# Another sequence and other rooms for the second part of an attention, dense and soft-MoE kernel

## The chip, the cores and the metric

The kernel runs on one core of one Trainium2 chip. The metric is the device time of one execution in microseconds (us).

## The reference

Three layers stand one behind the other.

- Attention in which a query sees only the keys of its own cluster. The shapes are 2 batches, 8 heads, 768 tokens, 64 columns, with 16 centroids per head. Query and key are each assigned to the centroid with the largest cosine.
- A dense layer on 1536 tokens x 512 columns: `h = x @ w_in` (512 x 2048), `g = h * clip(h + 3, 0, 6) / 6`, `x = g @ w_out` (2048 x 512).
- A soft mixture of 8 experts with 4 slots each: logits by `phi` (512 x 32), a softmax over the tokens for the input of the slots, two matrices per expert (512 x 1024 and 1024 x 512, relu between), and a softmax over the slots for the output.

```python
logits = x @ phi
d = np.exp(logits - logits.max(0, keepdims=True)); d /= d.sum(0, keepdims=True) + 1e-09
slot_input = d.T @ x                                  # 32 slots x 512
slot_out[e] = np.maximum(slot_input[e] @ w1[e], 0.0) @ w2[e]
c = np.exp(logits - logits.max(1, keepdims=True)); c /= c.sum(1, keepdims=True) + 1e-09
return (c @ slot_out).astype(np.float32)              # 1536 x 512
```

## The kernel before

Batch and head make 16 heads in all (head 8 to 15 belong to batch 1), and the tokens make 12 tiles of 128 (tile 6 to 11 belong to batch 1). The heads run one after the other; the dense layer of a tile can only start when all heads of its batch are done. So the dense layer of batch 0 runs beside the heads of batch 1, and the dense layer of batch 1 behind the heads.

Every piece of the work is a Python generator that issues instructions up to its next `yield`; such a stretch is a step. `ev` (L270) numbers the generators, and `flush` (L273) issues all steps in the sequence of `ORDER`, a list of 2706 numbers of generators written out as text: the n-th time that a number stands there, the n-th step of that generator is issued. Each engine executes its own instructions in the order in which they were issued, and the DMA queues of SP and ScalarE take their transfers in that order too. The text `ORDER` is thus the order of work on every engine. `Rooms` (L206) gives a tile a fixed buffer among those of its kind by its name: `ROOMS` lists `name:number`; a new tile in a room waits until the readers of the former one are done. A tile whose name has no number, or another text than the others, gets a buffer of its own kind.

The generators of which this document speaks are these; `name(arguments)` with a number behind it (`.4`) is the step, counted from 0.

- `keep(n, m)` (L374) issues m filler matmuls of 256 columns (L377) into a tile kw that nobody reads.
- `cast_lo` (L427, transfer at L443) turns the low part of query and key of a head with a DMA on SP's queue; `as_mm` (L461, L467) multiplies the turned tile by the centroids. `maxr`, `scores`, `maxq` and `as_put` are other steps of a head.
- `hid(t, fb, part, parts)` (L745) multiplies tile t by a fourth of `w_in`; `act(t, f0, f1)` (L748) computes the dense layer's function on ScalarE, VectorE and GpSimd (L762, L764, L358, L368), and its step `.4` turns the result with a DMA on SP's queue (L773), or for tiles 6, 10 and 11 with TensorE (L782). `logits(t)` (L790, matmuls at L796 and L797) reads the turned tile; it is called the classifier of tile t here.
- `colmax`, `dweights`, `dispatch` (L814 to L862) keep a running softmax over the tokens and the input of the slots; `zsum` (L1246), `slot_in` (L1281) and `slot_t` (L1290) finish that input.
- `fetch` (L1048) issues the transfers of the experts' weights on SP's queue, two halves of 512 KB per number (`fetch4.1` is the second half of number 4; L1099), each into a room of memory that earlier tiles leave. The second matrices of the last four experts come in two parts of 352 and 160 columns (`PARTS`, L1057), of which the output's first and second part are made. The first fetches read `wos`, the converted `w_out`, which is stored to memory from ScalarE's queue before.
- `combine_weights` (L1304) computes the softmax over the slots on VectorE, ScalarE and GpSimd, and turns it in its step `.11` with twelve transposes of TensorE (L1340).
- `layer1` (L1408), `relu`, `turn` (L1432), `layer2` (L1447) and `layer2_part(p, i)` (L1462) are the experts' layers; `layer2_part` also scales its result (ScalarE L1474, VectorE L1476).
- `combine(p, b)` (L1368) makes the output of part p and batch b: matmuls (L1387), an eviction per piece by ScalarE (L1395) or VectorE (L1393), and the output transfers (L1398, L1401), of batch 0 on ScalarE's queue and of batch 1 on SP's.

Of the kernel before, what the change touches and what calls it, by code (L numbers as in the profile page):

```python
# [71 lines left out]
    "753 598 989 661 633 634 595 599 629 602 661 722 976 599 603 988 989 712 976 723 714 630 634 603 977 994 718 "  # L72
    "989 630 662 715 635 989 637 638 977 719 996 716 717 720 631 755 755 756 977 933 997 667 978 978 638 668 995 "
    "978 979 604 998 639 1002 632 632 636 636 640 1002 605 649 756 721 605 1002 1002 650 641 640 1000 724 642 642 "
    "999 645 643 725 650 726 979 726 1001 756 646 713 651 727 646 1003 644 644 647 728 713 671 1003 672 728 729 648 "
    "648 731 665 652 652 713 757 732 732 1008 1003 666 735 1022 669 653 757 733 989 976 663 654 736 654 1010 757 "
    "757 739 1009 758 736 737 758 670 673 759 740 730 730 740 1003 674 734 741 734 743 759 675 676 744 744 745 1011 "
    "677 677 738 1016 1016 1023 1024 1025 747 760 738 742 990 1026 1027 748 748 678 761 1028 771 742 990 765 746 "
    "990 749 679 991 682 679 746 750 750 683 772 683 991 826 680 763 684 767 766 751 821 686 768 681 991 752 664 "
    "764 769 664 752 681 685 690 687 687 664 770 992 1022 691 773 685 694 774 992 992 691 698 688 692 762 695 695 "  # L80
    "775 696 689 1119 762 689 699 693 775 762 776 693 699 777 777 697 1037 780 1037 697 993 1012 700 781 784 788 "
    "993 781 1002 1003 701 701 778 1029 779 782 785 785 779 783 783 789 792 796 990 786 789 793 793 790 787 787 797 "
    "797 794 702 798 1014 791 1013 791 795 795 799 1016 1016 703 1004 1004 1004 1004 1025 703 1027 1026 1015 1017 "
    "799 800 1029 801 1049 1044 801 1037 1017 1030 1005 1016 1017 1046 1031 1005 1005 1006 1006 1017 1037 1045 1038 "
    "1047 1048 1006 1007 1051 1058 1017 1048 1018 1048 1041 1048 1039 1052 1050 1018 1032 1018 1019 1053 1019 1019 "
    "1053 1028 1033 1059 1048 1053 1048 1048 1020 1018 1040 1020 1031 1024 1020 1053 1060 1061 1060 1053 1042 1053 "
    "1021 1060 1062 1034 1007 1053 1060 1054 1054 1063 1035 1054 1068 1063 1035 1063 1063 1055 1055 1069 1060 1055 "
    "1056 1063 1070 1056 1071 1056 1021 1057 1072 1043 1070 1023 1070 1036 1054 1070 1064 1064 1064 1073 1078 1109 "
    "1064 1033 1065 1073 1073 1073 1079 1065 1065 1109 1070 1066 1066 1066 1081 1073 1067 1032 1080 1080 1080 1057 "
    "1082 1074 1074 1074 1088 1080 1083 1083 1074 1034 1075 1083 1075 1089 1083 1075 1076 1076 1076 1067 1091 1110 "  # L90
    "1090 1090 1077 1080 1083 1092 1090 1084 1084 1090 1077 1084 1090 1090 1085 1093 1085 1085 1093 1093 1098 1111 "
    "1036 1093 1086 1086 1086 1099 1100 1090 1101 1101 1099 1087 1102 1101 1101 1093 1084 1093 1093 1099 1099 1104 "
    "1087 1101 1103 1105 1103 1103 1105 1103 1094 1099 1110 1094 1105 1094 1094 1099 1101 1099 1103 1095 1103 1105 "
    "1101 1095 1103 1105 1095 1105 1105 1106 1106 1106 1096 805 1127 1096 1096 1107 1107 1097 1097 1107 1108 1108 "
    "1133 1133 1106 1108 1133 1134 1143 1143 1133 1126 1143 1143 1143 1132 1135 1112 1112 1137 1139 1143 1140 1143 "
    "1143 1143 1143 1143 1143 1141 1113 1113 1141 1114 1114 1130 1141 1115 1115 1116 1144 1145 1111 1150 1155 1156 "
    "1117 1116 1117 1118 1118 1136 1151 1159 1159 1138 1136 1138 1146 1147 1147 1146 1148 1149 1157 1158 1165 1165 "
    "1152 1153 1154 1154 1154 1154 1154 1149 1148 1153 1142 1152 1154 1154 1154 1154 1142 1160 1143 1160 1154 1154 "
    "1154 1154 1154 1154 1154 1154 1154 1154 1154 1161 1142 1166 1166 1161 1142 1142 1167 1162 1163 1168 1167 1168 "
    "1169 1169 1169 1173 1169 1171 1171 1171 1171 1172 1174 1171 1171 1171 1171 1172 1172 1172 1172 1174 1171 1172 "  # L100
    "1172 1172 1172 1174 1174 1177 1177 1177 1177 1177 1176 1120 1176 1125 1128 1123 1176 1176 1176 1121 1122 824 0 "
# [31 lines left out]
)  # L133

ROOMS = (
    "acc_0:1 acc_1:1 acc_10:1 acc_11:0 acc_12:0 acc_13:0 acc_14:0 acc_15:1 acc_2:0 acc_3:1 acc_4:0 acc_5:1 acc_6:1 "
    "acc_7:0 acc_8:0 acc_9:0 al_1:0 al_10:0 al_11:1 al_2:1 al_3:2 al_4:0 al_5:1 al_6:2 al_7:0 al_8:1 al_9:2 as_0:0 "
    "as_1:1 as_10:0 as_11:1 as_12:1 as_13:0 as_14:1 as_15:1 as_2:0 as_3:0 as_4:0 as_5:1 as_6:0 as_7:1 as_8:0 as_9:1 "
    "cTp:2 cm_0:0 cm_1:1 cm_10:0 cm_11:0 cm_12:0 cm_13:1 cm_14:1 cm_15:1 cm_2:0 cm_3:1 cm_4:1 cm_5:0 cm_6:0 cm_7:1 "
# [1404 lines left out]
```

## Time and profile before

| what | value |
| --- | --- |
| median of 3 runs | 443.02 us (442.69 to 443.47) |
| profiled execution | 442.37 us |
| span of its instructions | 440.5 us, so 1.87 us lie around it |
| granted TensorE clock over the span | 0.997 |

One execution was taken by the profiler; the median belongs to three other ones. A time in a row is counted from the start of the span. PE is TensorE, PEld its weight loads, DVE VectorE, ACT ScalarE, POOL GpSimd, SP the engine that only issues transfers; ACTq and SPq are the queues on which transfers are issued. The duration of a matmul in a row contains its way through the array, so successive matmuls overlap, and what one takes of the engine is the distance from its start to the next one's. `Lnnn` is a line of the kernel, `a<-b` says that tile a is written from tile b, `xN` is a number of instructions, and what stands in square brackets at the end of a row of a timeline is the idle time of the engine before it and what ended it. The DMA share of a stretch is the mean busy share of the core's 16 DMA engines; it can come out a little over 1.

### The profile page before, as it was taken

To read this page: it belongs to the slowest core of one execution; us is meant where nothing else is said; L and a number is where in the kernel's file an instruction comes from. 1 tells how busy PE (TensorE), PEld (TensorE's weight loads), DVE (VectorE), ACT (ScalarE), POOL (GpSimd) and SP (SyncE) were. 2 spreads that over 40 slices of the span, in tenths; PEclk is the share of its full clock that TensorE was granted. 3 is DMA by queue.
4 is the path that set the end of the run, shared out by engine and by line. 5 is a ranking of instruction groups with operands and counts; after the bars stand their busy time and mean duration, and the time that the engine had idled before them with its cause. 6 is when DMAs were issued, how large, how long until landed. Compare 5 with 4: busy or idle time off the path is not lost.

```text
span 440.5 us, 11801 instructions
## 1 busy us (share of the span) xinstructions
PE 423.7 (96%) x4906; PEld 276.4 (63%) x4906; DVE 271.4 (62%) x479; ACT 310.5 (70%) x508; POOL 248.9 (57%) x213
## 2 busy tenths in 40 slices
PE   7899999999999999999999999999999999989993
PEld 5577778776887556565656566765454445652652
DVE  5999999999867678465577476713343344650322
ACT  7799999997999887888878788885344454510112
POOL 6557588966566586568776779887133323310000
PEclk9999999999999999999999999999999999999998
DMA  7998958996795999425884607975998997999998
GB/s 258 294 199 215 259 91 223 224 237 233 244 214 99 246 256 220 130 53 107 136 208 92 172 9 214 239 257 106 207 343 181 271 220 252 329 350 400 373 306 274
DMA packets 129909, 96.28 MB, mean 219 GB/s; under 512 B 99648, under 2 KB 115008, under 8 KB 129856
## 3 DMA queue, kind: packets, MB, share of 16 engines
q1 hardware_dynamic: 125936, 89.74, 79.6%
q10 hardware_dynamic: 3920, 5.80, 3.7%
q8 instruction: 38, 0.62, 0.6%
q14 instruction: 15, 0.12, 0.1%
HBM read 64.06 MB, written 7.34 MB: 162 GB/s over the span
## 4 chain that ended last, share of the span: by engine, by line
PE 74%; DVE 12%; ACT 6%; DMA 5%; issue 2%; ACTq 0%; SPq 0%; DVEq 0%
PE h L745 28%; PE st L591 6%; PE sm L553 6%; PE st L595 5%; DMA wk<-in_moe_w_dram 5%; DVE mxs L569 5%; PE acc L661 4%; PE acc L674 3%; PE acc L667 2%; PE acc L666 2%; PE z L853 2%; PE kw L377 1%; PE lg L796 1%; PE e L1408 1%; PE e1b L1408 1%
## 5 line engine op out<-in xcount | busy, mean ns | idle before, releaser
L368 POOL TENSOR_TENSOR pp<-p,pp 128x768 f16<-128x768 f32 x72 | 118.4, 1653 | 47.0 <-ACT pp L358 35.4
L745 PE MATMUL h<-wq,xt 128*128 128x512 f16 x576 | 134.7, 379 | 0.0
L569 DVE TENSOR_REDUCE mxs<-sm 128x1 f32<-128x768 f32 x96 | 89.2, 952 | 20.7 <-PE sm L553 19.9
L745 PEld LDWEIGHTS <-xt 128*128 128x128 f16 x576 | 54.2, 98 | 59.5 <-issue 3.4
L368 POOL TENSOR_TENSOR ghl<-r,ghl 128x1024 f16<-128x1024 f32 (+1 forms) x25 | 50.3, 2014 | 56.5 <-ACT ghl L358 50.8
L639 ACT ACTIVATE p<-st 128x768 f32<-128x768 f32 x72 | 58.2, 811 | 18.2 <-PE st L595 14.2
L358 ACT ACTIVATE pp<-p 128x768 f16<-128x768 f32 x72 | 60.4, 842 | 2.8 <-PE acc L674 1.8
L764 DVE SCALAR_TENSOR_TENSOR r<-r,h 128x1024 f32<-128x1024 f32 (+1 forms) x26 | 29.5, 1136 | 14.7 <-ACT r L762 14.4
L591 PE MATMUL st<-qk1t 128*128 128x384 f16 x144 | 35.1, 325 | 2.3 <-DVE qk2t L578 0.6
L762 ACT ACTIVATE r<-h,b_relu 128x1024 f32<-128x1024 f32 (+1 forms) x26 | 27.1, 1048 | 14.4 <-POOL ghl L368 8.3
L358 ACT ACTIVATE ghl<-r 128x1024 f16<-128x1024 f32 (+1 forms) x26 | 25.6, 986 | 15.9 <-DVE r L764 9.5
L667 PE MATMUL acc<-v,pp 128*128 128x64 f16 x432 | 36.1, 194 | 0.0
L666 PE MATMUL acc<-v,pp 128*128 128x65 f16 x432 | 36.1, 192 | 0.0
L661 PE MATMUL acc<-v,pp 128*128 128x65 f32 x288 | 35.6, 273 | 0.0
L661 PEld LDWEIGHTS acc<-v,pp 128*128 128x128 f32 x288 | 34.7, 192 | 0.9
L595 PE MATMUL st<-qk2t 102*128 102x384 f16 x144 | 35.2, 325 | 0.0
L553 PE MATMUL sm<-qk2t 80*128 80x384 f16 x144 | 34.4, 325 | 0.6 <-ACT wot L989 0.2
L666 PEld LDWEIGHTS <-pp 128*128 128x128 f16 x432 | 31.5, 99 | 2.9
L368 POOL TENSOR_TENSOR pr<-pr,pr 128x768 f16<-128x768 f32 x15 | 25.1, 1676 | 12.2 <-ACT pr L358 7.5
L667 PEld LDWEIGHTS <-pp 128*128 128x128 f16 x432 | 29.2, 96 | 2.8
L358 ACT ACTIVATE pr<-pr 128x768 f32<-128x768 f32 (+2 forms) x32 | 26.3, 823 | 3.0 <-DMA pr<-in_k_dram 1.3
L674 PE MATMUL acc<-v,pp 128*128 128x65 f16 x432 | 24.9, 193 | 0.0
(229 smaller groups left out, 802.6 us busy)
## 6 DMA issues: line engine op xcount, KB each, us to landing
wk<-in_moe_w_dram SPq DMA_DIRECT2D x33, 512.0 KB, 6.0
wi<-in_moe_w_in_dram SPq DMA_DIRECT2D x16, 512.0 KB, 6.1
wod<-in_moe_w_out_dram SPq DMA_DIRECT2D x16, 512.0 KB, 4.8
pr<-in_moe_w_dram SPq DMA_DIRECT2D x14, 512.0 KB, 7.4
wos<-wo ACTq DMA_DIRECT2D x8, 512.0 KB, 3.6
wk<-wos SPq DMA_DIRECT2D x8, 512.0 KB, 5.0
wk<-in_moe_w_dram SPq DMA_DIRECT2D x10, 352.0 KB, 7.8
pr<-in_q_dram SPq DMA_DIRECT2D x16, 192.0 KB, 4.2
```

The lines of the kernel that those rows point to most:

```text
L358: nc.scalar.activation(out, in_, AF.Copy, scale=scale)
L368: (nc.vector if e == "v" else nc.gpsimd).tensor_tensor(out=out, in0=in_, in1=hi, op=ALU.subtract)
L553: nc.tensor.matmul(s[:, j, 0:384], d["qk2t"][0:80, n, 0], d["qk2t"][0:80, 3 * j : 3 * j + 3, 1], start=True, stop=True,)
L569: nc.vector.tensor_reduce(out=mxs[i % 2][:, 96 + n : 97 + n], in_=s[:, :, 0:384], op=ALU.max, axis=AX.XY)
L591: nc.tensor.matmul(s[:, j, 0:384], d["qk1t"][:, t, 1], d["qk1t"][:, 3 * j : 3 * j + 3, 0], start=True, stop=False)
L595: nc.tensor.matmul(s[:, j, 0:384], d["qk2t"][0 : 96 + NT, t, 1], d["qk2t"][0 : 96 + NT, 3 * j : 3 * j + 3, 0], start=False, stop=True,)
L639: nc.scalar.activation(p32, s[:, :, 0:384], AF.Exp, scale=sc_exp)
L661: nc.tensor.matmul(o, p32[:, j, r * P : (r + 1) * P], d["v32"][:, t], start=(t == 0 and n == 0), stop=False)
L666: nc.tensor.matmul(o, hi, v1[:, t, 0:65], start=(t == 0 and n == 0), stop=False)
L667: nc.tensor.matmul(o[:, 0:64], hi, v1[:, t, 65:129], start=False, stop=False)
L674: nc.tensor.matmul(o, pl[:, j, r * P : (r + 1) * P], v1[:, t, 0:65], start=False, stop=False)
L745: nc.tensor.matmul(s[:, fb % 2], xt[:, lhs], wq[fb][:, hl, kk], start=(n == 0), stop=(n == 11))
```

## The change

Only the two texts change. `ORDER` keeps its 2706 numbers, each as often as before; its entries 1207 to 1893, from the last heads of batch 1 up to the end of the combinations, stand in another sequence (645 of these 687 places hold another number). `ROOMS` gives 96 names another room; the rooms of the fetched weights stay. No instruction is added, removed or altered.

What moves, read out of both texts:

- `keep(31)`, `keep(26)` and `keep(47)`, which stood among the steps of heads 14 and 15, stand behind the hidden layer of tile 11 or later: `keep(51)` and `keep(31)` now stand behind `dweights(10)`, `keep(48)` and `keep(49)` on either side of `dweights(11)`, `keep(60)` behind `slot_in`, `keep(26)` ahead of `combine(0, 0)`, `keep(47)` ahead of `combine(1, 1)`; none stands between `slot_t` and `layer1` any more.
- `as_mm(15)` stands earlier, by 5.3 us of TensorE's work, with the steps that prepare it. On SP's queue `cast_lo(15).1` stood ahead of `fetch0.0` and `act(3, 2, 4).4` and stands behind `fetch0.0`, `fetch1.0` and `act(3, 2, 4).4`. The last store of `wos` (`wout(3, 1, 2).1`, ScalarE's queue) stands earlier; `fetch0` and `fetch1` read `wos`.
- Among the steps of heads 13 to 15, scores, maxima and what follows them change places on all engines. The turns of `xtrans` come in the order of tiles 7, 10, 11, 8, 9 (before: 7, 10, 8, 9, 11).
- On SP's queue `fetch4.1` and `fetch10.1` now stand between `act(7, 0, 2).4` and `act(7, 2, 4).4`, with 23 halves ahead of the latter (before 22); `fetch8.1` stands between `act(8, 0, 2).4` and `act(8, 2, 4).4`, `fetch16.0` between `act(9, 0, 2).4` and `act(9, 2, 4).4`. Ahead of `act(8, 0, 2).4` stand 26 halves (before 27), ahead of `act(9, 0, 2).4` 28 (before 30), ahead of tile 11's hidden layer 33 in both. Behind that, `fetch21.1`, `fetch27.1` and `fetch30.1` change places with neighbours.
- `combine_weights.11` (the twelve transposes) stood between `slot_in` and `slot_t.1` and stands between `layer2_part(0, 0)` and `layer2_part(0, 1)`; the steps of `combine_weights` ahead of it on VectorE, ScalarE and GpSimd stand behind `zsum.3`, `slot_t`, `relu` and `turn`. `selectors` stands earlier, `turn(1, 1)` behind the first step of `layer2`.
- At the end `layer2_part(1, 1).0` stands ahead of `combine(0, 1).0` (before behind it), and `combine(0, 0).8`, the output transfer of batch 0's third piece, stands behind `combine(0, 1).5` and `layer2_part(1, 1).2` on ScalarE's queue.

Cut to the first lines of the sequence and to rooms of the tail:

```diff
@@ ORDER @@
-    "753 598 989 661 633 634 595 599 629 602 661 722 976 599 603 988 989 712 976 723 714 630 634 603 977 994 718 "
-    "989 630 662 715 635 989 637 638 977 719 996 716 717 720 631 755 755 756 977 933 997 667 978 978 638 668 995 "
...
+    "753 598 989 661 633 634 595 599 629 602 661 722 976 599 603 988 989 712 976 723 714 630 634 603 977 994 637 "
+    "630 933 989 715 635 631 995 977 755 976 716 1022 989 717 604 638 977 638 639 605 1023 996 978 669 670 978 997 "
...
@@ ROOMS @@
...
-    "kw_22:0 kw_23:1 kw_24:0 kw_25:0 kw_26:0 kw_27:0 kw_28:2 kw_29:1 kw_3:1 kw_30:1 kw_31:1 kw_32:1 kw_33:2 kw_34:0 "
-    "kw_35:1 kw_36:2 kw_37:0 kw_38:0 kw_39:2 kw_4:0 kw_40:1 kw_41:0 kw_42:2 kw_43:0 kw_44:2 kw_45:2 kw_46:0 kw_47:1 "
-    "kw_48:2 kw_49:2 kw_5:1 kw_50:0 kw_51:1 kw_52:1 kw_53:2 kw_54:1 kw_55:0 kw_56:0 kw_57:2 kw_58:1 kw_59:0 kw_6:2 "
-    "kw_60:0 kw_7:2 kw_8:1 kw_9:0 late_a0:0 late_a1:2 late_b0:4 lg_0:1 lg_1:0 lg_10:1 lg_11:1 lg_2:1 lg_3:1 lg_4:0 "
-    "lt_8:0 lt_9:0 mx2_0:0 mx2_1:1 mx2_10:0 mx2_11:1 mx2_12:0 mx2_13:1 mx2_14:0 mx2_15:1 mx2_2:0 mx2_3:1 mx2_4:0 "
+    "kw_22:0 kw_23:1 kw_24:0 kw_25:0 kw_26:2 kw_27:0 kw_28:2 kw_29:0 kw_3:1 kw_30:1 kw_31:1 kw_32:1 kw_33:2 kw_34:0 "
+    "kw_35:1 kw_36:2 kw_37:0 kw_38:0 kw_39:2 kw_4:0 kw_40:1 kw_41:0 kw_42:2 kw_43:0 kw_44:2 kw_45:2 kw_46:0 kw_47:0 "
+    "kw_48:0 kw_49:1 kw_5:1 kw_50:0 kw_51:2 kw_52:1 kw_53:2 kw_54:1 kw_55:0 kw_56:0 kw_57:2 kw_58:2 kw_59:0 kw_6:2 "
+    "kw_60:0 kw_7:2 kw_8:1 kw_9:0 late_a0:2 late_a1:0 late_b0:4 lg_0:1 lg_1:0 lg_10:0 lg_11:0 lg_2:1 lg_3:1 lg_4:1 "
+    "lt_8:1 lt_9:1 mx2_0:0 mx2_1:1 mx2_10:0 mx2_11:1 mx2_12:0 mx2_13:1 mx2_14:0 mx2_15:None mx2_2:0 mx2_3:1 mx2_4:0 "
-    "nt_o0_0:1 nt_o0_1:2 nt_o1_0:2 nt_o1_1:0 nt_o2_0:2 nt_o2_1:1 nt_o3_0:2 nt_o3_1:1 o2_0:0 o2_1:1 p32_0_1:0 "
+    "nt_o0_0:1 nt_o0_1:2 nt_o1_0:2 nt_o1_1:0 nt_o2_0:2 nt_o2_1:1 nt_o3_0:2 nt_o3_1:1 o2_0:1 o2_1:0 p32_0_1:0 "
-    "po_0_0_1:1 po_0_0_2:2 po_0_1_0:0 po_0_1_1:1 po_0_1_2:2 po_1_0_0:0 po_1_0_1:1 po_1_1_0:0 po_1_1_1:1 pp_0_0:2 "
+    "po_0_0_1:1 po_0_0_2:2 po_0_1_0:0 po_0_1_1:1 po_0_1_2:2 po_1_0_0:1 po_1_0_1:0 po_1_1_0:1 po_1_1_1:2 pp_0_0:2 "
...
```

## Rows read from the trace of the kernel before

**Rows 1.** Page, first part: busy us, share of the span, instructions.

```profile
span 440.5 us, 11801 instructions
...
PE 423.7 (96%) x4906; PEld 276.4 (63%) x4906; DVE 271.4 (62%) x479; ACT 310.5 (70%) x508; POOL 248.9 (57%) x213
```

**Rows 2.** By stage: length, busy (instructions) of five engines, clock, DMA share, GB/s.

```profile
241.00:302.00 61.00, 60.95 (x863) 40.78 (x861) 32.44 (x58) 49.92 (x79) 52.29 (x35) 1.00 0.64 166
302.00:379.00 77.00, 77.00 (x611) 39.06 (x610) 30.49 (x51) 35.35 (x69) 27.28 (x15) 1.00 0.99 246
379.00:395.40 16.40, 14.32 (x224) 9.29 (x220) 10.94 (x29) 6.43 (x20) 3.01 (x11) 1.00 0.98 335
395.40:409.20 13.80, 13.79 (x128) 4.06 (x128) 0.69 (x1) 1.18 (x2) 0.00 (x0) 1.00 1.02 399
409.20:425.30 16.10, 16.10 (x244) 10.61 (x242) 3.49 (x8) 1.19 (x3) 0.00 (x0) 1.00 1.07 358
425.30:440.50 15.20, 7.81 (x90) 4.81 (x84) 4.96 (x7) 4.25 (x7) 0.00 (x0) 0.92 0.84 269
```

**Rows 3.** The same view, the stretch of the output.

```profile
429.00:438.00 9.00, 4.40 (x54) 3.02 (x46) 3.08 (x5) 2.94 (x5) 0.00 (x0) 1.00 1.03 343
```

**Rows 4.** Fillers (tile kw), 241 to 379 us: ns min/median/max, first, last start.

```profile
L377 PE MATMUL kw<-ident,ident x6: 270/270/274, 277.2 to 284.7; 128*128 128x256 f16 x6
```

**Rows 5.** TensorE's timeline around 277 us: start, duration, what.

```profile
277.17 0.38 PE L377 MATMUL kw<-ident,ident 128*128 128x256 f16 x2
277.39 0.81 PE L553 MATMUL sm<-qk2t 80*128 80x384 f16 x4
```

**Rows 6.** Timeline of TensorE at two readers of turned tiles.

```profile
261.32 0.45 PE L467 MATMUL as<-ct,qk1t 128*128 128x32 f16 x12
...
339.81 0.19 PE L796 MATMUL lg<-wp,gt 128*128 128x64 f16 x1
```

**Rows 7.** Landing of turns: L443, 180:262 us; L773, 334:336 and 353:354 us.

```profile
DMA to landing us min/median/max: 3.8/3.8/4.6
...
DMA to landing us min/median/max: 4.3/4.3/4.3
...
DMA to landing us min/median/max: 7.6/7.6/7.6
```

**Rows 8.** Timeline of SP's DMA issues, 326 to 365 us.

```profile
328.59 7.67 SPq L773 DMA_TRANSPOSE gt<-ghl  x2
...
334.33 1.93 SPq L773 DMA_TRANSPOSE gt<-ghl  x1
...
349.11 1.89 SPq L1099 DMA_DIRECT2D wk<-in_moe_w_dram  x3
```

**Rows 9.** Timeline of TensorE around 393 us.

```profile
393.01 0.84 PE L1340 MATMUL cTp<-ident,late_a 128*128 128x128 f16 x12
393.95 1.08 PE L1298 MATMUL sit<-i,zacc 128*128 128x32 f32 x8
```

**Rows 10.** Timeline of VectorE around 393 us.

```profile
393.15 0.75 DVE L1292 TENSOR_SCALAR zacc<-si,rs 128x512 f32<-128x512 f32 x1 [0.79 <-PE si L1281]
```

**Rows 11.** Timeline of TensorE, 425 to 431 us.

```profile
425.33 0.44 PE L1462 MATMUL o<-pr,late_w 128*32 128x160 f32 x4
...
429.90 0.46 PE L1387 MATMUL po<-late_a,late_a 128*128 128x352 f16 x2 [0.25 <-ACT late_gt L1395]
430.29 0.84 PE L1462 MATMUL o<-wk,late_w 128*32 128x160 f32 x16
```

**Rows 12.** Chain of waits of 405 to 441 us, in order of time.

```profile
419.94 6.11 DMA wk<-in_moe_w_dram
```

**Rows 13.** Timeline of ScalarE and its DMA issues, 425 to 434.5 us.

```profile
428.08 0.91 ACTq L1398 DMA_DIRECT2D out_dram<-late_w  x2
...
429.88 0.38 ACTq L1398 DMA_DIRECT2D out_dram<-late_gt  x1
...
431.16 0.39 ACT L1474 ACTIVATE late_a<-o,mask 128x160 f16<-128x160 f32 x1
```

98 rows, old and new, of tables (ORDER, ROOMS) are left out of this document.

## The prediction

> **What bounds the kernel now.** I read the page's first part before anything else, then a table of busy time by stage, then the timelines of single stages, and the chain of waits and the DMA landings last. The first part shows TensorE busy for 423.7 of 440.5 us, far ahead of ScalarE with 310.5 [rows 1]. That share is a mean over stages with different limits, so the table by stage decides [rows 2]. From 241 to 302 us (heads 13 to 15 beside the dense layer of the tiles of batch 0) TensorE is busy 60.95 of 61.00 us, from 302 to 379 us (the dense layer of batch 1) 77.00 of 77.00, and no other engine there is over 52.29. A step that leaves its queue there brings everything behind it forward, provided that what it waits for is early enough; a step that other engines do there costs nothing until TensorE waits for it. From 379 to 395.4 us TensorE is busy 14.32 of 16.40 us: a chain of short steps over ScalarE, VectorE and TensorE ends the dense layer. From 395.4 to 425.3 us it is full again (13.79 of 13.80 and 16.10 of 16.10) and the DMA engines are full too (shares of 1.02 and 1.07). From 429 to 438 us the DMA engines write the output at a share of 1.03 while TensorE is busy 4.40 of 9.00 us [rows 3]: there the end is set by when the first output transfer starts and by its bytes, not by what any engine does later.
>
> **The sum's base.** The profiled execution took 442.37 us, 0.65 below the median of 443.02. I take differences against the profiled one and add them to the median. About 0.2%, 0.9 us, is what a measurement of this kernel can tell from no change, so the band of no change is 442.1 to 443.9.
>
> **Fillers that leave the full stretch.** Before, the stretch of the last heads holds six filler matmuls of 256 columns, three `keep` steps [rows 4]. One takes 0.22 us of TensorE's time: it starts at 277.17 and the next operation at 277.39 [rows 5]. The new order puts none there and has them, and the others, behind token tile 11's hidden layer, in pauses that the chain from 379 to 395.4 us leaves and between the last combinations. Every hidden layer from tile 8 on thus stands behind 0.66 us less of matmuls. Gain: 3 x 0.22 = 0.66 us. Bounds: 0, if they stood over waits that now come out as waits, to 0.66. I take 0.66, since 60.95 of 61.00 us leaves room for no wait that a filler is needed for.
>
> **The rest of that stretch.** Head 15's centroid product moves forward by some 5.3 us of TensorE's work, from 261.32 us [rows 6]. The transfer that turns its input moves with it on SP's queue; it now stands behind two weight fetches and one more turn that it preceded. I count its input ready in time with about 2 us to spare, at a landing of 3.8 us after issue [rows 7]: cost 0. If the cover goes, TensorE waits by what the transfer is late. The maxima and scores of heads 13 to 15 change places on VectorE, ScalarE and GpSimd, all of which have over 8 us of slack in the 61 us [rows 2]: cost 0, with the same condition. The last store of the converted output weights, on ScalarE's queue, moves forward; the first two fetches wait for it, so this delays nothing: 0. In the tail, three halves of weights (21.1, 27.1, 30.1) change places on SP's queue with neighbours of the same size, where the DMA engines are full: 0, bounds 1.3 us either way, the time of 512 KB at the 399 GB/s of that stage [rows 2]; I take 0, as the bytes stay.
>
> **Fetches past turns on SP's queue.** SP issues both the turns of the dense layer's activations and the fetches of 512 KB. Two fetches more than before (4.1 and 10.1) stand ahead of the second turn of tile 7; one stands between the two turns of tile 8 and one between those of tile 9. A fetch that waits for its room holds up the turn behind it, and one that has been issued shares the DMA engines with it. Before, tile 7's second turn is issued at 334.33 us [rows 8] and lands 4.3 us later, at 338.6 [rows 7]; the classifier of tile 7 reads it at 339.81 [rows 6]. Slack: 1.2 us. Behind three fetches, issued from 349.11 us on, the first turn of tile 9 took 7.6 us to land [rows 7, 8], 3.3 more. Bounds: 0, if the fetches are through by then, to 3.3 - 1.2 = 2.1 us. I take 0, nearest to the 4.3 us: between its two turns of tile 7, issued at 328.59 and 334.33, SP issues nothing else [rows 8], and the two fetches, if their rooms are free, fill these 5.7 us.
>
> **The tail.** The twelve transposes of the combination weights (line 1340) run before at 393.01 us, while VectorE scales the slots' input; TensorE's next step, which reads the scaled tile, starts at 393.95 [rows 9, 10]. Taken out there, they free nothing, since the next step waits for VectorE anyway. In the new order they follow the first part of `layer2_part(0, 0)`, in the stretch with 16.10 of 16.10 us busy [rows 2], where they push everything back. Cost: a filler of 256 columns takes 0.11 us, so 128 columns take about 0.055, and 12 of them 0.66 us. Bounds: 0, if TensorE waits for weights there, to the 0.84 us of the row. Against a wait: the last weights of the first output part are read in a row of matmuls without a gap up to 425.33, and the chain of waits shows a weight transfer ending at 426.05, in the second part's matmuls [rows 11, 12]; the pushed step ends the first part, whose result goes over ScalarE and VectorE to the first combination. I take 0.66. The vector steps of the weights move behind `slot_t`, `relu` and `turn`, where VectorE is busy 0.69 of 13.80 and 3.49 of 16.10 us [rows 2]: cost 0.
>
> **The order at the end.** On ScalarE's queue the transfer of the third piece of batch 0 (0.38 us of issuing, at 429.88) moves behind batch 1's middle eviction and the scaling at 431.16 [rows 13]. From this row alone the term is -0.38. But the scaling waits for the sixteen matmuls that start at 430.29, and these stand behind a combination that starts at 429.90 when a PSUM room comes free [rows 11]; and what follows is written by DMA engines that are full from 429 to 438 us [rows 3]. I take 0, bounds -0.38 to 0. The Trainium skill, page "DMA: Bandwidth & Descriptors", section "Issuing engines are not separate DMA queues", says that transfers started by different engines run on the same sixteen DMA engines and interleave, and that only issue time is at stake. By that rule the term is 0, by the issuing row it would be -0.38; the share of 1.03 sides with the rule.
>
> **Sum.** -0.66 + 0 + 0 + 0.66 + 0 = 0.0 us: 443.0 us.
>
> **Rivals.**
> *Faster: both gains are kept.* The transposes fall into a wait for weights (the chain runs through weight transfers up to 426.05 [rows 12], and those move forward with the body), and the end of ScalarE's queue counts in full: -0.66 - 0.38 = -1.04, 442.0 us. For it: the DMA pieces end so close to their use. Against: the gapless matmuls, and the full DMA engines at the end.
> *Slower: a turn comes late.* Tile 7's second turn lands behind the fetches 4.1 and 10.1. With two of the three fetches that cost 3.3 us, it is 2.2 us later, 1.0 past its slack, so TensorE, which takes its steps in order, stands for 1.0 us; with all of the 3.3 it stands for 2.1. That gives 443.0 + 1.0 = 444.0 to 445.1, say 444.2 us. It decides from a landing time of 5.5 us on (4.3 + 1.2). For it: turns are the transfers that a queue of fetches stretches (three were issued at 349.11, just ahead of the 7.6 us). Against: the fetches may be issued long before.
> *The fillers covered waits.* Then the gain is 0 and the transposes cost 0.66: 443.7 us, inside the band. Against: the busy time.
> *The clock falls.* The granted clock is 1.00 in every stage up to 425.3 us and 0.92 over the last one [rows 2], the fall coming after the last matmul. Were it at half for the matmuls of the last stage, the 0.84 us of sixteen second-layer matmuls [rows 11] and the like would take about twice as long, some 1.3 us in all on the chain: 444.3 us. The Trainium skill, page "TensorE: Matmul & The Clock Gate", Part 1, states that half clock is the default state and that activity releases it, which speaks against taking fillers away. In the body the engine is never idle, so by that rule nothing changes there; no row of before shows the rest.
>
> **How the numbers follow.** Chances: forecast 0.42, faster rival 0.20, late turn 0.20, covered waits 0.13, clock 0.05. The forecast and the covered waits lie within the band: 0.55; faster 0.20; slower 0.25. The range runs from 441.9, just below the faster rival, to 444.6, which takes in the late turn with up to 1.6 us of waiting and the clock; below and above lie the ends of the bounds.
>
> **What the changed profile would show.** Right: TensorE full from 241 to 379 us with no filler in it; tile 11's last hidden matmul some 0.66 us earlier; the transposes in a gapless row near 422 us; `layer2_part(0, 1)` ending within 0.2 us of 425.6 and the DMA engines full to within 0.3 us of 438. Wrong: a gap ahead of tile 7's, 8's or 9's classifier with a turn as its releaser; one ahead of head 15's centroid product; a second-layer matmul that waits for a weight transfer; a clock below 1.00 before 430 us; a first output transfer issued much earlier than 428.08 [rows 13].

## The result, and the profile after

| kernel | median of its runs | ratio to the kernel before | 95% interval |
| --- | --- | --- | --- |
| before, beside it | 443.04 us | | |
| changed | 449.23 us (446.80 to 451.05) | 1.0138 | 1.0119 to 1.0158 |

The changed kernel is slower by 6.2 us; the forecast was 443.0 us, no change. The profiled execution took 451.05 us, the slowest of its six. Ratios are taken over the undisturbed runs of both kernels and are not the quotients of the medians.

The page's first part of the changed kernel says little: TensorE is again at 96%, with 5.6 us more of busy time for the same instructions.

```profile
span 449.2 us, 11798 instructions
...
PE 429.3 (96%) x4906; PEld 278.5 (62%) x4906; DVE 271.1 (60%) x479; ACT 309.5 (69%) x508; POOL 249.2 (55%) x213
```

The table by stage answers to [rows 2]; the last four stages are cut where the same steps stand, so they begin 5.5 to 8 us later than before. Columns as there.

```profile
241.00:302.00 61.00, 61.00 (x848) 40.42 (x847) 32.55 (x61) 50.34 (x78) 52.43 (x34) 1.00 0.64 161
302.00:384.50 82.50, 79.52 (x632) 39.99 (x631) 30.66 (x51) 35.39 (x70) 28.58 (x16) 0.98 1.00 236
384.50:400.90 16.40, 13.91 (x209) 8.74 (x205) 7.83 (x21) 5.93 (x19) 3.01 (x11) 1.00 0.90 308
400.90:414.80 13.90, 13.86 (x128) 4.06 (x128) 1.39 (x4) 1.19 (x2) 0.00 (x0) 1.00 1.01 365
414.80:433.26 18.46, 18.30 (x256) 11.66 (x254) 5.73 (x14) 1.59 (x3) 0.00 (x0) 1.00 1.04 357
433.26:449.20 15.94, 9.14 (x98) 5.31 (x90) 4.96 (x7) 4.20 (x7) 0.00 (x0) 0.95 0.82 260
```

The stage of heads 13 to 15 is as full as before. The dense layer of batch 1 took 77.00 us without a pause and now takes 82.5, with 2.98 us of idle time and a mean clock of 0.98. The chain and the first experts' layer are as long as they were. The stage up to the first part's end took 16.1 us and takes 18.5. Two places, then: one in the dense layer, one in the tail.

The place in the dense layer is one wait. TensorE's timeline of the changed kernel, in the middle of tile 7's classifier, answers to [rows 6]:

```profile
340.96 0.18 PE L797 MATMUL lg<-wp,gt 128*128 128x32 f16 x1
344.07 0.20 PE L796 MATMUL lg<-wp,gt 128*128 128x64 f16 x1 [2.94 <-DMA gt<-ghl]
...
344.52 4.44 PE L745 MATMUL h<-wq,xt 128*128 128x512 f16 x12
```

The first half of the classifier reads tile 7's first turn, the second half the second turn, and that lands 3.1 us late. The second cost is in the last row: the twelve matmuls behind the wait take 4.4 us from 344.52 to 348.91, where they took 2.7 before (340.69 to 343.38). The stretches of that place show why (columns as above, the clock third from the end):

```profile
341.20:344.07 2.87, 0.00 (x0) 0.00 (x0) 0.00 (x0) 0.00 (x0) 0.25 (x1) 1.00 1.18 200
344.07:346.00 1.93, 1.93 (x22) 1.04 (x23) 0.34 (x2) 1.20 (x2) 0.00 (x0) 0.80 0.94 318
346.00:348.00 2.00, 2.00 (x6) 0.70 (x5) 1.17 (x1) 0.80 (x1) 0.00 (x0) 0.50 0.99 381
348.00:349.00 1.00, 1.00 (x5) 0.55 (x4) 0.00 (x0) 0.26 (x1) 0.66 (x1) 0.68 2.81 222
```

Behind 2.87 us without a matmul the granted clock falls to half, 1.2 GHz, and comes back before 349 us: 0.80, 0.50 and 0.68 in the three stretches, which is 0.39 + 1.00 + 0.32 = 1.7 us of full clock lost. The engine counts as busy all that time: 1.7 of the 5.6 us of additional busy time are these slow matmuls, no work. The Trainium skill, page "TensorE: Matmul & The Clock Gate", Part 1, has half clock as the default state which activity releases. This trace agrees in that the clock is 1.00 again while the engine works without a pause; that it falls after every such pause is not so, as b_sp_after shows below.

Why the turn is late is read on SP's queue. Its timeline in the changed kernel answers to [rows 8]:

```profile
321.35 4.63 SPq L729 DMA_TRANSPOSE xt<-xhl  x1
326.03 5.04 SPq L1099 DMA_DIRECT2D wk<-in_moe_w_dram  x3
331.24 4.28 SPq L773 DMA_TRANSPOSE gt<-ghl  x1
335.56 0.58 SPq L1099 DMA_DIRECT2D pr<-in_moe_w_dram  x1
336.19 0.43 SPq L1099 DMA_DIRECT2D wk<-in_moe_w_dram  x1
336.72 5.26 SPq L773 DMA_TRANSPOSE gt<-ghl  x1
342.03 0.58 SPq L1099 DMA_DIRECT2D pr<-in_moe_w_dram  x1
```

and the landing times of the two halves (fetch4.1, fetch10.1) and of the second turn, from issue, are

```profile
DMA to landing us min/median/max: 5.3/5.6/6.0
...
DMA to landing us min/median/max: 7.3/7.3/7.3
```

A turn alone takes 1.93 us to issue [rows 8]. Here one holds the queue for 5.26 us, from 336.72 to 341.98, and fetch10.1, issued at 336.19, lands 6.0 us later at 342.2. The turn itself lands at 344.0, about 2 us behind. The first turn, too, holds the queue for 4.28 us, to 335.52. It keeps the two halves from being issued in the 5.7 us that the forecast had given them.

And that first turn is issued only at 331.24. The three fetches ahead of it take 5.04 us to issue; the waits of SP's queue (us in total, times, longest) of 318 to 345 us show one, the second line, for the last turn of the normalised input:

```profile
SPq L773 <- POOL ghl L368: 10.5, 2, 5.8
SPq L1099 <- DMA xt<-xhl: 3.5, 1, 3.5
```

It is fetch14.0, whose room is memory of that input; issued at 330.74 us, it lands at 335.70, and the first turn lets go of the queue at 335.52. Before, it stood behind both turns of tile 7.

The first of the two lines could be read as a late input from GpSimd. For tile 7's second turn it is not: GpSimd had finished that input at 335.69 us, 1.0 us before the turn is issued, and the view puts the wait down to GpSimd's next work, which ends at 341.45 and belongs to tile 8.

```profile
333.56 2.13 POOL L368 TENSOR_TENSOR ghl<-r,ghl 128x1024 f16<-128x1024 f32 x1 [3.57 <-ACT ghl L358]
```

The place in the tail, on TensorE's timeline of the changed kernel (answers to [rows 9, 11]):

```profile
429.54 0.84 PE L1340 MATMUL cTp<-ident,late_a 128*128 128x128 f16 x12
430.31 2.04 PE L1462 MATMUL o<-wk,late_w 128*32 128x352 f32 x22
432.50 1.07 PE L1462 MATMUL o<-wk,late_w 128*32 128x352 f32 x9 [0.16 <-DMA wk<-in_moe_w_dram]
```

The transposes stand in the full stretch, and behind them a second-layer matmul waits for a weight transfer.

Step by step, the start of the same step in the two profiled executions gives the account (changed minus before): +1.15 us at the hidden layer of tile 3, where both kernels still have the same sequence (the difference arises in the first 32 us and belongs to the execution, not to the change); -0.52 to tile 6's hidden layer; +0.10 to tile 8's; +3.11 in the wait; +1.69 in the slow matmuls; +0.37 between `turn` and `layer2_part(0, 0)`; +1.45 with the transposes and the weights behind them; +0.59 in the second part, +0.59 up to the first combination, -0.05 to the last one. Sum: 8.5 us of the 8.7 by which the spans differ; the rest lies behind the last combination.

The medians differ by less, 6.2 us, so the profiled execution is not a typical one. Of the six runs of the changed kernel the three with a mean clock of 0.993 to 0.996 took 449.84 to 451.05 us, the three with 0.997 and 0.998 took 446.80 to 448.61. A loss of 1.7 us is 0.004 of the span, so this fits a fall of the clock in some executions only; the other five have no trace, and it is not shown.

### The profile page after: what moved, and what is told of

The parts are those of the page before. It is cut to its first block, busy times and chain, and to the rows that moved or that the text cites. A ratio compares the mean times of both kernels' runs of the same rounds, so it can differ in the third digit from the quotient of the medians.

```text
span 449.2 us, 11798 instructions
## 1 busy us (share of the span) xinstructions
PE 429.3 (96%) x4906; PEld 278.5 (62%) x4906; DVE 271.1 (60%) x479; ACT 309.5 (69%) x508; POOL 249.2 (55%) x213
## 4 chain that ended last, share of the span: by engine, by line
PE 69%; DVE 11%; DMA 9%; ACT 6%; issue 2%; POOL 2%; SPq 0%; ACTq 0%; DVEq 0%; POOLq 0%
PE h L745 25%; PE st L591 5%; PE st L595 5%; PE sm L553 5%; DVE mxs L569 4%; PE acc L661 4%; DMA wk<-in_moe_w_dram 4%; PE acc L674 3%; PE acc L666 2%; PE acc L667 2%; DMA pr<-in_moe_w_dram 2%; PE kw L377 2%; PE z L853 2%; DMA gt<-ghl 2%; DMA qk1t<-pr 1%
## 5 line engine op out<-in xcount | busy, mean ns | idle before, releaser
L745 PE MATMUL h<-wq,xt 128*128 128x512 f16 x576 | 136.2, 382 | 0.0
```

What stands on the lines that cost most here:

```text
L745: nc.tensor.matmul(s[:, fb % 2], xt[:, lhs], wq[fb][:, hl, kk], start=(n == 0), stop=(n == 11))
```

## The experiments

An experiment edits the text of `ORDER`, and of `ROOMS` where that is said. The diffs name the steps in place of their numbers. "Before" is the kernel before, run beside each on the same chip (medians 442.8 to 443.4 us).

**Two halves put back** (a_two_back). On the changed kernel:

```diff
  act(7, 0, 2).4
- fetch4.1
- fetch10.1
  act(7, 2, 4).4
+ fetch4.1
+ fetch10.1
  fetch6.1  fetch11.1  fetch9.1
  act(8, 0, 2).4
```

> The new kernel with two halves of weights (fetch4.1 and fetch10.1) put back behind the second turn of tile 7 on SP's queue; nothing else differs. Theory (the turn is late): the new kernel's TensorE waited 3.1 us for this turn ahead of and inside tile 7's classifier, and the twelve matmuls behind the wait took 1.7 us more at half clock. Both go, 4.8 us: 449.2 - 4.8 = 444.4 us, clock 1.00 from 302 to 379 us. Rival (the transfers as a whole are late): the weights' stream sets the end, so that taking the wait away lets TensorE wait for weights later: not under 448 us. Second rival (the wait moves on): tile 8's second turn, still behind fetch8.1, is late next: about 446 us with a gap ahead of tile 8's classifier.

Measured: 451.44 us (450.16 to 451.76), ratio 1.0183 [1.0162, 1.0205]. The wait at tile 7 is gone, and a longer one stands at tile 8's classifier; TensorE's timeline has

```profile
356.02 0.24 PE L796 MATMUL lg<-wp,gt 128*128 128x64 f16 x1 [3.39 <-DMA gt<-ghl]
```

The second rival is right in kind and too small in size. SP's queue shows five halves ahead of tile 8's first turn now, and the turn holds the queue for 8.15 us:

```profile
338.86 0.92 SPq L1099 DMA_DIRECT2D wk<-in_moe_w_dram  x2
340.81 8.15 SPq L773 DMA_TRANSPOSE gt<-ghl  x1
349.01 0.58 SPq L1099 DMA_DIRECT2D wk<-in_moe_w_dram  x1
349.63 4.29 SPq L773 DMA_TRANSPOSE gt<-ghl  x1
```

**Four halves put back** (a_four_back), that is fetch8.1 and fetch16.0 too, so that no half stands between two turns of a tile:

```diff
  act(8, 0, 2).4
- fetch8.1
  act(8, 2, 4).4
+ fetch8.1
...
- fetch16.0
  act(9, 2, 4).4
+ fetch16.0
```

> The same, and fetch8.1 and fetch16.0 are put behind the second turns of tiles 8 and 9 as well. Theory (the turn is late): no turn has a fetch between it and its partner, no classifier waits: 444.4 us or a little less, since the tail's steps are those of the new kernel. If the wait only moves on to tile 8 in the run above, this one shows it: 444.4 against about 446 us. Rival (the transfers as a whole are late): not under 448 us.

Measured: 446.92 us (446.61 to 448.81), 1.0090 [1.0070, 1.0111]. Still a wait at tile 8, now of 2.0 us:

```profile
355.35 0.20 PE L796 MATMUL lg<-wp,gt 128*128 128x64 f16 x1 [1.95 <-DMA gt<-ghl]
```

and on SP's timeline

```profile
341.41 11.41 SPq L773 DMA_TRANSPOSE gt<-ghl  x2
```

The expectation missed: halves between the turns are not needed for a late turn. The row joins tile 8's two turns. The first holds the queue for 9.38 us, to 350.79, until the last of the five halves ahead has landed (350.92); the second, whose input was ready at 347.13, can only be issued then.

**One fetch put back** (a_14_back), the one that had waited for its memory:

```diff
- fetch14.0
  act(7, 0, 2).4
  fetch4.1  fetch10.1
  act(7, 2, 4).4
+ fetch14.0
```

> The new kernel with one transfer moved: fetch14.0 goes from ahead of tile 7's first turn to behind tile 7's second. In the new kernel's trace fetch14.0 is issued at 330.74 us, right after the last turn of the normalised input landed at 330.69 (its room is that memory), and tile 7's first turn only behind it, at 331.24. Theory (a chain on SP's queue: a fetch that waits for its room holds the first turn, that turn holds the queue until what is ahead of it has landed, so the two halves and the second turn go out late): the first turn goes out near 329.4, the second lands near 340, the gap of 3.1 us in tile 7's classifier shrinks to under 0.5 us; with fetch14.0 more fetches stand ahead of tile 8's first turn, so 1 to 3 us may come back at tile 8's classifier: 444.5 to 447.5 us. Rival (the two halves between the turns do it alone): the gap stays at 2 us or more.

Measured: 447.16 us (446.25 to 449.37), 1.0089 [1.0062, 1.0115]. SP's timeline:

```profile
328.49 2.95 SPq L773 DMA_TRANSPOSE gt<-ghl  x1
331.49 0.58 SPq L1099 DMA_DIRECT2D pr<-in_moe_w_dram  x1
332.11 0.43 SPq L1099 DMA_DIRECT2D wk<-in_moe_w_dram  x1
334.19 3.46 SPq L773 DMA_TRANSPOSE gt<-ghl  x1
...
338.80 0.90 SPq L1099 DMA_DIRECT2D wk<-in_moe_w_dram  x2
340.11 7.58 SPq L773 DMA_TRANSPOSE gt<-ghl  x1
```

The first turn goes out at 328.49, and tile 7's second turn, with the same two halves ahead of it, is issued 2.5 us sooner (1.5 of these because this execution runs earlier: its classifier starts at 339.02, the changed kernel's at 340.54) and lands at 339.4 (5.2 us from issue); tile 7 does not wait at all, so the theory holds against the rival. The wait of tile 8 is 2.50 us here, with one half more ahead of its first turn. The last two halves ahead of that turn are issued from 338.80 on, and the later of them lands at 347.8, as the turn lets go of the queue (340.11 + 7.58 = 347.7).

**The whole of SP's sequence, in both directions.** In a_sp_before the changed kernel gets the former sequence of fetches and input turns on SP's queue; in b_sp_after the kernel before gets the new one. Of the first the part around tile 7 is

```diff
- fetch12.0  fetch13.0  fetch14.0
+ fetch11.0  fetch12.0  fetch12.1
  act(7, 0, 2).4
- fetch4.1  fetch10.1
  act(7, 2, 4).4
- fetch6.1  fetch11.1  fetch9.1
+ fetch1.1  fetch13.0  fetch14.0  fetch10.1  fetch14.1
  act(8, 0, 2).4
...
```

> The new kernel with the fetches and the turns of the normalised input (xtrans) set back, from as_put(15).1 to fetch17.0, to the sequence that SP's queue had before; all other steps stand as in the new one. Theory (SP's sequence makes the waits): no classifier waits, clock 1.00; the body keeps the 0.66 us of the fillers; what is left is the new tail, +0.7 to +1.9 us: 443.2 to 444.5 us. Rival (the sequence of the computing steps makes the turns late): a gap of 1 us or more ahead of tile 7's or 8's classifier, over 446 us.

> The kernel before with the fetches and xtrans turns set, from as_put(15).1 to fetch17.0, in the new kernel's sequence; close2, which issues nothing and frees memory for fetch14, moves with them; computing steps as before. Theory (SP's sequence makes the waits): a gap of 2 to 3.5 us in the classifier of tile 7 or 8 and 1 to 1.7 us at half clock behind it: 446 to 448.5 us. Rival (the computing steps' sequence): 443 to 444 us with no such gap.

Measured: a_sp_before 444.58 us (444.16 to 447.07), 1.0040 [1.0021, 1.0060]; b_sp_after 446.79 us (442.47 to 449.36, the runs lie all over that range, three of the twelve below 443.3), 1.0053 [1.0026, 1.0080]. Their rows for the dense layer of batch 1 and for tile 7's classifier:

```profile
302.00:379.00 77.00, 76.93 (x613) 38.99 (x612) 30.11 (x49) 35.46 (x70) 27.83 (x16) 1.00 0.99 246
```

is a_sp_before, full at clock 1.00; and b_sp_after has

```profile
344.50 0.20 PE L796 MATMUL lg<-wp,gt 128*128 128x64 f16 x1 [3.38 <-DMA gt<-ghl]
```

In the profiled execution SP's sequence alone makes the wait, in a kernel whose computing steps are the former ones, and taking it away removes the wait from the changed kernel. The three runs of b_sp_after that are as short as the kernel before make it likely that the wait does not come in every execution; they have no trace. In b_sp_after the matmuls behind the wait ran at full clock, so that part of the expectation missed:

```profile
341.00:344.50 3.50, 0.12 (x6) 0.01 (x2) 0.00 (x0) 0.00 (x0) 0.60 (x1) 1.00 1.09 289
344.50:346.50 2.00, 2.00 (x24) 1.17 (x25) 0.42 (x2) 1.31 (x3) 0.00 (x0) 1.00 1.00 379
```

**Two halves put forward in the kernel before** (b_two_fwd).

```diff
  act(7, 0, 2).4
+ fetch1.1
+ fetch13.0
  act(7, 2, 4).4
- fetch1.1
- fetch13.0
```

> The kernel before with two halves (fetch1.1 and fetch13.0) moved forward on SP's queue to stand between the two turns of tile 7; nothing else differs. Theory (the turn is late): SP issues the halves as soon as the first turn lets go of the queue, near 334 us, the second turn holds the queue until both have landed near 339.5 us and lands near 341.5, 1.7 us after its use at 339.8: a wait of 1 to 2.5 us and up to 1.7 us at half clock, so 444.0 to 447.2 us, with the gap in tile 7's classifier. Rival (the turn alone is not enough; the new sequence of the heads ahead of it makes it late): no gap, 443.0 us.

Measured: 444.02 us (442.16 to 447.35), 1.0025 [1.0003, 1.0047]; the profiled execution, 442.54 us, has no gap there. With the first turn early (issued at 328.82 us) the halves go out at 332.2 and 332.8 and the turn lands at 339.5, 0.6 us before the classifier starts. The hold is there (the second turn issues for 3.27 us, the later half lands at 337.6), but the halves go out 3.4 us earlier than in the changed kernel. So two halves between the turns do not suffice for a wait, and that the median lies in the theory's range is no support for it: in the trace the rival's sign, no gap, is what came. Two of twelve runs took over 446 us; whether the wait came in those is not shown, as they have no trace.

**TensorE given work in the wait** (a_hid_first). On the changed kernel:

```diff
+ hid(9, 0, 0, 1).0
  logits(7).0
  ...
- hid(9, 0, 0, 1).0
  colmax(7).0
```

> The new kernel with the first twelve matmuls of tile 9's hidden layer (hid(9, 0), 2.6 us of TensorE's work) ahead of tile 7's classifier instead of behind it; SP's queue as in the new kernel. Theory (TensorE waited and only then lost its clock): the gap shrinks from 3.1 to about 0.5 us and no matmul runs at half clock there, -4.3 us in the profile's terms: 445 us, if the wait does not come back at tile 8, whose second turn landed 0.5 us ahead of its use when all was 5.5 us late; if it comes back there, 447 to 449 us. Rival (transfers as a whole set the end): 448 to 450 us with waits for weights in layer2_part.

Measured: 449.06 us (445.46 to 451.02), 1.0113 [1.0074, 1.0152]. The wait for the turn is gone at tile 7; two waits for the classifier's next steps (0.60 and 0.47 us) and one at tile 8 for its turn (0.85 us from one matmul's start to the next one's) take its place. From tile 8's hidden layer to tile 10's the execution loses 2.3 us against the kernel before, where the changed kernel loses 4.8. Over its runs that gain is not seen: a start of 4.0 us later, ahead of the first changed step, went into the profiled one, in which the granted clock is 0.86 from 13 to 21 us and 0.88 from 21 to 40, where the kernel before and the changed kernel have 1.00. The run is inconclusive on the total.

**The fillers alone** (b_fill_out). On the kernel before:

```diff
- keep(31, 2).0   - keep(26, 2).0   - keep(47, 2).0
...
  keep(29, 2).0
+ keep(31, 2).0   + keep(26, 2).0   + keep(47, 2).0
```

> The kernel before with the three filler steps keep(31), keep(26) and keep(47) taken from the stretch of the last heads and put behind the last matmul; nothing else differs. By the forecast's first term each frees 0.22 us of a full TensorE: 443.0 - 0.66 = 442.4 us. Rival (they covered waits): 443.0 us, with gaps of 0.2 us where they stood.

Measured: 442.75 us (441.76 to 443.67), 0.9990 [0.9977, 1.0003]. By the starts of the steps the first two give 0.64 us, 0.47 come back as short waits ahead of `dweights(3)` and `scores(14, 4)` between 281 and 283 us, and the third gives 0.22: 0.37 us in all. Between the two theories, nearer to the gain.

**The transposes alone** (b_ctp), on the kernel before.

```diff
  slot_in(3).0
- combine_weights.11
  slot_t.1
...
  layer2_part(0, 0).1
+ combine_weights.11
  layer2_part(0, 1).0
```

> The kernel before with the twelve transposes of the combination weights, and the copy behind them, moved behind layer2_part(0, 0). Forecast's term: +0.66 us, 443.85 us, with the first combination 0.66 later. Rival (they fall into a wait for weights): 443.2 us. A second: TensorE's next step at 393 us starts earlier without them: 0.1 us less.

Measured: 443.68 us (443.12 to 444.84), 1.0011 [1.0001, 1.0021], that is +0.5 us. TensorE's timeline:

```profile
394.31 0.85 PE L1298 MATMUL sit<-i,zacc 128*128 128x32 f32 x6 [0.87 <-DVE zacc L1292]
```

```profile
423.04 0.47 PE L1462 MATMUL o<-wk,late_w 128*32 128x352 f32 x2
423.44 0.84 PE L1340 MATMUL cTp<-ident,late_a 128*128 128x128 f16 x12
424.21 2.57 PE L1462 MATMUL o<-wk,late_w 128*32 128x352 f32 x32
```

Where they stood, a wait of 0.87 us for VectorE takes their place, as forecast. Where they now stand, the steps behind them are 0.91 us later.

**The tail alone** (b_new_tail, b_new_tail2). The former body, and from tile 11's hidden layer on the new sequence and rooms.

```diff
  (ORDER up to act(10, 2, 4).2 as before)
- (the rest in the former sequence)
+ (the rest in the new sequence; ROOMS of its tiles new)
```

> The kernel before up to tile 11's hidden layer, and from there on its steps in the new sequence and in the new rooms; the three fillers stay in the body. Between the first layer of the experts and the last combination the new kernel loses 2.95 us more than the one before, a_four_back 1.9. Theory (the tail itself costs only the twelve transposes, the rest are weights that came late because the body was late): +0.7 to +0.9, 443.9 to 444.1 us. Rival (the tail's sequence costs all of it): +1.9 to +2.95, 445.1 to 446.1 us, with waits for weights in layer2_part.

Measured: 447.08 us (445.78 to 448.03), 1.0095 [1.0078, 1.0112], but with a gap of 1.5 us inside tile 11's hidden layer, which neither kernel has: a room of the new tail was still taken by a tile of the former body. The run does not answer its question; the next one does.

```diff
- gp_10_2:1 lt_9:0 z_9:0
+ gp_10_2:0 lt_9:1 z_9:1
```

> As b_new_tail (the former body, the new sequence and rooms from tile 11's hidden layer on), with the room of the turned tile gp_10_2 also taken from the new kernel: in b_new_tail the new room of h_11_3 was that of the former gp_10_2, so tile 11's last hidden matmuls stood 1.5 us behind an eviction, a seam of the experiment. Theory (the tail's own cost is the transposes, the order of turn and layer2, and weights late for the second part): no gap at the seam, last combination 1.2 to 1.8 us later: 444.4 to 445.0 us. Rival (b_new_tail's 447.1 is the tail itself): over 446 us.

Measured: 444.59 us (443.32 to 445.63), 1.0032 [1.0017, 1.0046], no gap at the seam. By the starts of the steps: 0.27 us between `turn` and `layer2_part(0, 0)`, 0.89 with the transposes, 0.22 in the first part, 0.40 up to the first combination: 1.8 us, the theory's upper end.

**The new body with the former SP sequence and the former tail** (a_sp_b_tail), an edit of a_sp_before:

```diff
- (from tile 11's hidden layer on: the new sequence and rooms)
+ (the former ones; keep(31), keep(26), keep(47) behind the last matmul)
```

> The kernel a_sp_before (the new body with SP's former sequence) with the tail, from tile 11's hidden layer on, in the former sequence and rooms; the three fillers stay out, behind the last matmul. Theory (the new body without SP's change is worth the fillers, the tail costs 1.7 us of its own): 444.6 - 1.7 = 442.9 us or down to 442.5, level with or a little under the kernel before. Rival (the tail's loss came from the body): no change from a_sp_before, 444.4 us.

Measured: 442.37 us (441.67 to 445.94), beside 443.38 for the kernel before; 0.9984 [0.9966, 1.0003]. Against a_sp_before the last combination is 1.8 us earlier with respect to the same body, so the tail costs that much here as well. Of all kernels run this is the fastest, but its interval reaches 1, so it is not shown to beat the kernel before.

## Why the prediction was wrong

The forecast of 443.0 us and the range up to 444.6 both failed on the step **Fetches past turns on SP's queue**, in its sentence that the two fetches, "if their rooms are free, fill these 5.7 us". In the changed kernel they could not. The forecast took the 5.7 us between the issues of tile 7's two turns for an empty queue. The row of 7.67 us in [rows 8] joins both turns; taken apart, it is 3.19 us in which the first turn holds the queue,

```profile
328.59 3.19 SPq L773 DMA_TRANSPOSE gt<-ghl  x1
```

2.55 us in which the queue is free because the second turn's input is not ready, and 1.93 us of the second turn. That is room enough for two halves (b_two_fwd), as long as the first turn is early.

In the changed kernel it was not. Its input was ready at 329.99 us, but fetch14.0, ahead of it, waited for its room until 330.74; the turn was issued at 331.24 and held the queue for 4.28 us, up to the landing of fetch14.0. So the halves went out at 335.56 and 336.19, and the second turn, whose issue moved from 334.33 to 336.72 us, held the queue until they had landed. (Its input, too, was ready later, at 335.69 instead of 334.30; the classifier starts 0.73 us later than before.) The landing time of 7.3 us against the 7.6 that had set the bound was no surprise. The prediction names the mechanism, "a fetch that waits for its room holds up the turn behind it", and gave it no cost: I counted the halves ahead of the second turn (23 instead of 22) and not which of them waits, and for what. a_14_back, which moves fetch14.0 alone, takes the wait of tile 7 away, and so does a_two_back, which moves the two halves alone: the wait needed both.

**The rival "a turn comes late"** had the mechanism, the place and the sign, at a chance of 0.20 and a price of 1.0 to 2.1 us. Measured in the profiled execution: 3.1 us, and 1.7 more for the clock. I had priced the clock as a rival of its own, in the last stage only; it came as a consequence of the wait. And with a_two_back, a_four_back and a_14_back the price turns out to belong to SP's whole sequence: each repair of tile 7 moved the wait to tile 8 (3.39, 1.95 and 2.50 us), because the fetches put back stand ahead of the next turn. Of the sequences tried in the changed kernel only the former one (a_sp_before) has no wait of that size.

**Fillers that leave the full stretch**: right in size for the new sequence. The changed kernel gains 0.52 us up to tile 6's hidden layer, a_sp_before 0.51 there and 0.63 up to tile 8's, against 0.66. Taken out of the former sequence alone they gave 0.37, because one of them stood over waits: the rival "the fillers covered waits" was partly right for that sequence.

**The rest of that stretch**: right. Head 15's centroid product runs at 257.15 us and its turn had landed at 254.9; the stage is 61.00 of 61.00 us busy.

**The tail**: right in its reading, mis-sized in the sum. Taken out at 393 us the transposes free nothing; put into the full stretch they cost 0.9 us instead of 0.66: 0.77 from their first to the next matmul and the rest between them and the matmul ahead. Two costs were not in the sum. `turn(1, 1)` behind the first step of `layer2` costs 0.27 us, and I had not costed it. And b_new_tail2 loses 0.22 us in the first output part and 0.40 up to the first combination. Its trace has no filler ahead of that combination, and a_sp_before, which has one, loses as much, so the filler is not needed for this loss. Weights that land later are: the second-layer matmul that was released by a weight transfer at 426.05 us [rows 12] is released by one at 427.90 in b_new_tail2. As that is 1.85 us, these weights could set the tail's whole loss even without the transposes; no run separates the two. The two terms lie within the bound of 1.3 us that the changed places of fetches were given. Together the new tail costs 1.8 us on its own, 2.95 in the changed kernel, where TensorE also waits for a weight transfer ahead of 432.50. That the weights are late there because the fetches were held up behind the turns is likely (236 GB/s from 302 to 384.5 us against 246 before), but not isolated by a run.

**The order at the end**: consistent with 0. In a_sp_before the first and the last combination are as far apart as before to within 0.1 us; no run moves this transfer alone. That agrees with the Trainium skill, page "DMA: Bandwidth & Descriptors", section "Issuing engines are not separate DMA queues", by which only issue time is at stake. The same section of the Trainium skill calls the issue time usually small relative to the transfer; for a turn that stands behind other transfers this case shows 4.28 to 8.15 us of issuing, of 6.5 to 10.1 us until it lands, and the measurement decides.

The account closes without the wait: a_sp_before gains about 0.6 in the body, loses 0.2 at one turn of tile 8 and 1.8 in the tail, +1.4, and its median is 1.45 us over that of the kernel before. So without the wait the time, 444.58 us, would just have stayed inside the range, and the forecast would still have been 1.5 us too low, by the tail.

## What to carry to other kernels

On a queue that issues both plain transfers and turning ones, price a move by the queue's whole sequence: which transfer waits for its room, what stands behind that one, and until when each turn holds the queue. A step that is put back behind one user goes ahead of the next, so a repair has to be followed to the next reader. Where TensorE's wait is the cost, add what its clock may take afterwards.

## What was not expected of the hardware

A turn of the activations (L773) on SP's queue took 1.93 us to issue with nothing ahead of it and between 2.95 and 9.38 us behind other transfers; in the cases followed it let go of the queue within 0.3 us of the landing of the last one ahead (335.5 and 335.7, 342.0 and 342.2, 347.7 and 347.8 us), and its own data landed some 2 us later (3.6 in b_sp_after). The kernel before has this too, at no cost: tile 8's first turn holds the queue there from 340.92 to 346.96 us, and its reader starts at 352.13. The smaller turns of the normalised input (L729) do not behave so: in the changed kernel one is issued at 318.01 us and lets go at 319.61, while a load ahead of it lands at 326.1. What sets this apart is open.

TensorE's clock fell to 0.50 after 2.87 us without a matmul in the changed kernel and in a_two_back after a wait of 3.39 us; after one of 3.38 us in b_sp_after it stayed at 1.00, and so it did after the shorter ones of a_four_back (1.95 us) and a_14_back (2.50 us). In a_two_back the stretches around the wait were

```profile
352.50:356.02 3.52, 0.13 (x6) 0.02 (x2) 0.00 (x0) 0.00 (x0) 0.32 (x1) 0.90 1.21 189
356.02:358.00 1.98, 1.98 (x20) 1.15 (x21) 0.29 (x1) 1.12 (x2) 0.00 (x0) 0.50 0.60 205
```

So behind a pause of about 3 us the clock took between nothing and 1.7 us more, from one execution to another.
